# A linear attention and gated feed-forward kernel on one core: the diagonal term token-major from the seventh group on, a group's attention products in one visit of TensorE, two masked copies per group

## Chip, cores, metric

The kernel runs on one core of a Trainium2 chip. The metric is device time in microseconds (us) of one execution, lower is better. A core has TensorE (PE, matmuls; PEld is its weight load), VectorE (DVE), ScalarE (ACT), GpSimd (POOL) and SyncE (SP, which here issues every DMA).

## What is computed

Batch 4, 8 heads, 768 tokens, head width 48; r, k, v, w and u in float32, the feed-forward weights in float64. The reference, cut to what matters:

```python
for t in range(S):                                   # attention with a decaying state
    cur = einsum('bhd,bhe->bhde', u * k[t], v[t])    # the diagonal term: token t on itself
    y[t] = einsum('bhd,bhde->bhe', r[t], state + cur)
    state = w * state + einsum('bhd,bhe->bhde', k[t], v[t])
x = y laid out as (B, S, 384)
h = relu(x @ w_in)                                   # 384 -> 1024
gate = sigmoid(conv over 3 neighbouring tokens of h)
out = (h * gate) @ w_out                             # 1024 -> 384
```

## The kernel before, in words

**Attention.** Tokens go in chunks of C = 64 and groups of GT = 128 (two chunks); there are 6 groups per batch and NG = 24 in all, numbered g. The eight heads are four pairs (NP): one head of a pair lies on the upper partitions, the other on the lower ones, so most products come as two small matmuls side by side. Tiles with a number g % 3 hold three groups (NBUF).

For each group `prep` (L445) does this: it scales k and r in their channel-major form by powers of w (`KR`, on DVE); DMAs the scaled r into `RA` and `RB`, the moving operand of the output product; builds the diagonal term; and scales the token-major k, `KT`, into `KTA`/`KTB` (for g >= DK = 8 through an in-place product and two DMAs). The diagonal term of a token is the sum over the channels of r u k, one number for each token and head. Before, it comes in four steps: `KP` = k times r in channel-major form (512 columns, DVE or POOL); `qmm`, 32 matmuls of one column each that sum `KP` with the weights `uw` over the partitions into `psS` (L476 and L477); an ACT copy into `QQ`; and, for g >= DS = 2, a product of `QQ` with the identity `eye` that writes a diagonal matrix for all heads into `SC` (L298, class "dg").

`scores` (L504) makes the 64 x 64 products of k and r of a chunk in `psC` (32 matmuls, L513 and L514). For g >= DS one masked copy on DVE (COPY_PREDICATED, 128 partitions, L518) puts the part above the diagonal into `SC`, and two DMAs move `SC` into the two halves of `RA` and `RB`. For the first two groups POOL's affine_select (L498) writes the diagonal straight into `RA` and `RB`, and two masked copies of 64 partitions (L524) go there too.

`step(g, c)` (L529) is one chunk: `S`, the next state, 16 matmuls into `psS` (L536, L537), which two ACT copies take into `WW` (L543) where the next chunk's products read it; and `av`, the output of the chunk, 16 matmuls into `psY` (L550, L551). The last chunk of a batch has no `S`. `yout` copies `psY` out and lays it into `XT`, split into two float32r parts.

**Feed-forward.** 9 units of tokens (three of 254 to 258 in batch 0, then 384 each) times 8 blocks of 128 channels make 72 steps. `first` (L612, 9 matmuls into one of two `HP` banks) is followed by a chain that goes back and forth between ACT (ReLU L616, L617, sigmoid L623, rounding to `GH` L626) and DVE (two taps of the convolution L620, the gate L624), with the low part `GL` on DVE or POOL. `second` (L641, 9 matmuls into `PO`) comes three steps later. The weights arrive as float64 words and are turned into two float32r parts on ACT, DVE and POOL during the first third of the kernel.

**The order.** Every operation is entered in a `Plan` with an engine (or DVE and POOL to choose from, `tt("any", ...)`), an estimated duration and the tiles that it reads and writes. `late` gives each a due time, from the order of entry of PE's operations and a table of offsets OFF by class. `order` then schedules all of them on a model of the engines, earliest start first, most overdue first among those that are ready, and writes the instructions out in that order for each engine. For PE an operation of the kind in progress (feed-forward, or attention as a whole: ATT) gets a bonus of BON = 6 us, and leaving attention is charged SWITCH = 0.19 us. Groups are entered in `pieces`: at piece 3g `prep(g + 2)` and `scores(g + 1)`, then `step(g, 0)`, then `step(g, 1)`, `yout(g)` and `load(g + 3)`; so each third of a group is due at its own place between the feed-forward steps. In the steady part this gives visits of attention on PE such as q + av, S + sc and S + av, with feed-forward between them.

Of the kernel before, what the change touches and what calls it, by code (L numbers as in the profile page):

```python
# [5 lines left out]
F32 = mybir.dt.float32  # L6
# [4 lines left out]
ALU = mybir.AluOpType  # L11
# [2 lines left out]

DR = 2
DK = 8
DS = 2
LAG = 3
WPRE = 2
LEAD = 6  # L20
# [28 lines left out]
C = 64  # L49
# [13 lines left out]
class Plan:  # L63
# [6 lines left out]
    def __init__(self):  # L70
        self.ops = []
        self.last_w, self.last_r = {}, {}
        self.port = []

    def op(self, eng, dur, rd, wr, fn, cls="", x=0.0, port=False):
# [21 lines left out]
        self.port.append(port)  # L97
        return n

    def late(self):  # L100
        ops, n = self.ops, len(self.ops)
        late = [1e6] * n
        t = T0
        for i, (dur, x, pred, fn, cls) in enumerate(ops):
            if "pe" in dur and x:
                late[i] = t
                t += dur["pe"] * (1 + (SLOW if t < TS else 0.0))
        for i in reversed(range(n)):
            for j in ops[i][2]:
                d, x = ops[j][:2]  # L110
                m = min(d.values()) + LAT if "sp" not in d else d["sp"] + x + 1.5
                late[j] = min(late[j], late[i] - m)
        for i in range(n):
            late[i] -= OFF.get(ops[i][4], 0.0)
        return late

    def order(self):
# [17 lines left out]
        seq, where, when = [], [None] * n, [None] * n  # L135
        fill, hist = FILL, []
        lanes = [0.0] * 7
        att = False
        todo = n
        while todo:  # L140
            best = None
            for e in self.ENG:
                av = avail[e]
                if not av:
                    continue
                f = free[e]
# [12 lines left out]
                m = min(max(f, ready[i]) for i in av)
                lim = m + DELTA  # L160
                if e == "pe":
                    i = min((late[i] - (BON if (ops[i][4] in ATT) == att else 0.0), i) for i in av if ready[i] <= lim)[1]
# [8 lines left out]
            if e == "pe":  # L171
# [20 lines left out]
                if att and cls not in ATT:  # L192
                    free[e] += SWITCH
                att = cls in ATT
                s = max(s, free[e])
                k = int(s / self.TICK)
                if k > tick:
# [45 lines left out]


LAT, LPE = 0.18, 0.21
SLOWER, SHARED, SWITCH, XFER = 0.8, 1.25, 0.19, 1.45
ATT = ("th", "sc", "S", "av", "q")


def rwkv_ffn_kernel(tc, krd, krt, vt, wd, ut, w_in, conv_w, w_out, out):  # L250
# [4 lines left out]
    with ExitStack() as ctx:  # L255
# [11 lines left out]
        KTA, KTB = sb([112, NP, 2, D], F32, "KTA", NBUF), sb([128, NP, 2, D], F32, "KTB", NBUF)  # L267
        WW = sb([128, 2, NP, 2, D], F32, "WW", NBUF)
        WA, WB = [x[0:112, 0] for x in WW], [x[:, 1] for x in WW]
        KT = sb([128, NP, 2, D], F32, "KT", NBUF)  # L270
        KP = sb([112, NP, GT], F32, "KP", 2)
        QQ = sb([128, NP * 2], F32, "QQ", NBUF)
        YY = sb([128, NP, 2, GT], F32, "YY", 2)
# [19 lines left out]

        def tt(eng, n, rd, wr, cls="", **kw):
            d = {"dve": dve(n), "pool": pool(n)}
            if eng != "any":
                d = {eng: d[eng]}
            op(eng, d, rd, wr, lambda e: e.tensor_tensor(**kw), cls, port=True)  # L298
# [4 lines left out]

        wz = sb([128, 512], BF16, "wz")
        wc = sb([112, NP], F32, "wc")
        uc, uw = sb([112, NP], F32, "uc"), sb([112, NP], F32, "uw")
        mask = sb([128, C], I32, "mask")
        ident, eye = sb([112, D], F32, "ident"), sb([128, C], F32, "eye")
# [17 lines left out]
        if NW:  # L326
            op("pe", 0.2134 * NW, ["wz"], ["o2"], warm, "", 512 * NW)

        def load(g):
            i = g % NBUF  # L330
            dma([], [("KK", i), ("RR", i)], KR[i], krd[g], 0.45, 1.27, "ldK")
            dma([], [("KT", i)], KT[i], krt[g, :, 0], 0.45, 0.55, "ldT")
            dma([], [("Wv", i, "a")], WA[i][0:64], vt[g, 0:64, 0], 0.45, 0.27, "ldV")
            dma([], [("Wv", i, "b")], WB[i][64:128], vt[g, 64:128, 1], 0.45, 0.27, "ldV")

# [108 lines left out]

        def prep(g):  # L445
            i = g % NBUF
            k_t = KT[i]

            def c2(ap, n):
                return ap.unsqueeze(2).broadcast_to([n, NP, 2, C])  # L450
# [18 lines left out]
            kp = KP[g % 2]  # L469
            tt("any", 512, [("KK", i), ("RR", i)], [("KP", g % 2)], out=kp, in0=KK[i], in1=RR[i], op=ALU.mult)  # L470

            def qmm(e):
                for p in range(NP):
                    for c in range(2):
                        n, t = NP * D + 2 * p + c, slice(c * C, (c + 1) * C)
                        PE.matmul(psS[0:64, n:n + 1], kp[64:112, p, t], uw[64:112, p:p + 1], start=True, stop=True)  # L476
                        PE.matmul(psS[64:128, n:n + 1], kp[0:48, p, t], uw[0:48, p:p + 1], start=True, stop=True)  # L477
            op("pe", 0.4, [("KP", g % 2), ("uw", 0), ("uw", 64)], ["psAu", "psBu"], qmm, "q", 16)
            op("act", 0.2, ["psAu", "psBu"], [("QQ", i)], lambda e: A.copy(QQ[i], psS[:, NP * D:NP * D + 2 * NP]))
# [24 lines left out]
        def scores(g):  # L504
# [3 lines left out]
            def mm(e):  # L508
                for c in range(2):
                    for p in range(NP):  # L510
# [1 line left out]
                        n = (2 * p + c) * C  # L512
                        PE.matmul(psC[0:64, n:n + C], kk[64:112, p, t], rr[64:112, p, t], start=True, stop=True)  # L513
                        PE.matmul(psC[64:128, n:n + C], kk[0:48, p, t], rr[0:48, p, t], start=True, stop=True)  # L514
            op("pe", 0.5, [("KK", i), ("RR", i)], ["psAs", "psBs"], mm, "sc", 768)
            if g >= DS:
                sc = SC[g % 2].rearrange("q (a t) -> q a t", t=C)
                op("dve", 0.68, ["psAs", "psBs", "mask"], [("SC", g % 2)], lambda e: V.copy_predicated(  # L518
# [10 lines left out]
        def step(g, c):  # L529
            i = g % NBUF  # L530
            b, gi = divmod(g, GPB)
            if not (gi == GPB - 1 and c == 1):
                def smm(e):
                    for p in range(NP):
                        n = p * D
                        PE.matmul(psS[64:112, n:n + D], KTA[i][:, p, c, :], WA[i][:, p, c, :], start=True, stop=True)  # L536
                        PE.matmul(psS[0:48, n:n + D], KTB[i][:, p, c, :], WB[i][:, p, c, :], start=True, stop=True)  # L537
                j, cn = (i, 1) if c == 0 else ((i + 1) % NBUF, 0)
                op("pe", 0.2, [("KTk", i, "a"), ("KTk", i, "b"), ("KTd", i, "a", c), ("KTd", i, "b", c), ("KTd", i), ("Wv", i, "a"),
                              ("Wv", i, "b"), ("WS", i, c), ("Wz", i)], ["psAu", "psBu"], smm, "S", 720)  # L540
                for nm, T, ps, o in (("a", WA, psS, 64), ("b", WB, psS, 0)):
                    op("act", 0.21, ["psAu" if nm == "a" else "psBu"], [("WS", j, cn)] if nm == "a" else [("WS", j, cn)],
                       lambda e, T=T, ps=ps, o=o: A.copy(  # L543
                           T[j][o:o + 48, :, cn, :], ps[o:o + 48, 0:NP * D].rearrange("q (p d) -> q p d", p=NP)))
            t = slice(c * C, (c + 1) * C)

            def av(e):
                for p in range(NP):
                    n = p * GT + c * C
                    PE.matmul(psY[64:112, n:n + C], WA[i][:, p, c, :], RA[i][0:112, p, t], start=True, stop=True)  # L550
                    PE.matmul(psY[0:48, n:n + C], WB[i][:, p, c, :], RB[i][:, p, t], start=True, stop=True)  # L551
            op("pe", 0.25, [("Wv", i, "a"), ("Wv", i, "b"), ("WS", i, c), ("Wz", i), ("Rr", i, "a"), ("Rr", i, "b"), ("Rs", i, "a"), ("Rs", i, "b"), ("Rz", i)],
               ["psY"], av, "av", 960)

        def yout(g):
            b, gi = divmod(g, GPB)
# [203 lines left out]
```

## Time and profile before

| | |
|---|---|
| Runs of the kernel | 353.74, 355.93, 356.5 us; median 355.93 |
| The profiled execution | 356.31 us, its span on the core 354.6 us |
| Mean granted TensorE clock | 0.971 |
| Instructions | 10924 |
| DMA traffic | 46.62 MB in 28498 packets |

The profile is one execution taken by the hardware profiler. Times in it are us from the span's start, or ns where marked. A line of PE's timeline gives the start, the length, the line of the kernel, the operation and what it reads and writes; matmuls overlap, so the time that a series takes is read from start to start. A row of the groups gives line, engine, operation, shapes and count, then busy us and mean ns, then the engine's idle time ahead of them and what ended it. L298 is the helper `tt`, where nearly all elementwise products are issued, and L301 the helper for DMAs; there the tiles' names tell what it is.

### The profile page before, as it was taken

Reading aid. Unit: us, or ns where it says so; the run is one execution under the profiler, and the core shown is the slowest. Engines: PE = TensorE matmul, PEld = TensorE weight load, DVE = VectorE, ACT = ScalarE, POOL = GpSimd, SP = SyncE. Lnnn points to the kernel's source line nnn. Section 1 sums busy time; section 2 is a strip of 40 time slices with the busy share of each in tenths; the row PEclk is TensorE's granted clock in tenths of the full one; section 3 lists DMA queues with packets and bytes.
Section 4 is the critical chain, followed back from the end, with each engine's and each line's share of the span. In section 5 each row is a group of like instructions: output and inputs, shape, how many; then the busy total and the mean of one; then the engine's idle time right before and its main releaser. Section 6 shows DMA issues by size and latency. Waiting matters only on the chain.

```text
span 354.6 us, 10924 instructions
## 1 busy us (share of the span) xinstructions
PE 338.8 (96%) x4439; PEld 311.8 (88%) x4439; DVE 239.6 (68%) x387; ACT 215.4 (61%) x531; POOL 150.4 (42%) x159
## 2 busy tenths in 40 slices
PE   7899898859999999999999999999999999999996
PEld 3688787749999999999899999999989999999995
DVE  7969969898676777776765666566534665565560
ACT  5445685854575677465646674565555776676752
POOL 8878676397532224345326242424122031233330
PEclk9899989876999999999999999999999999999999
DMA  7947956776446436866655272457332300010101
GB/s 185 271 131 193 273 162 220 227 186 159 120 132 179 146 108 169 224 170 165 181 131 163 77 193 79 123 146 208 77 72 57 110 3 2 11 67 2 67 2 67
DMA packets 28498, 46.62 MB, mean 131 GB/s; under 512 B 5984, under 2 KB 18784, under 8 KB 28448
## 3 DMA queue, kind: packets, MB, share of 16 engines
q1 hardware_dynamic: 28448, 45.92, 47.3%
q8 instruction: 35, 0.57, 0.6%
q14 instruction: 15, 0.12, 0.1%
HBM read 26.77 MB, written 4.72 MB: 89 GB/s over the span
## 4 chain that ended last, share of the span: by engine, by line
PE 85%; DVE 8%; DMA 3%; issue 2%; ACT 2%; SPq 0%; DVEq 0%
PE PO L641 30%; PE HP L612 29%; PE psY L550 6%; PE psC L513 5%; PE psS L476 5%; PE psS L536 5%; PE PO L696 2%; DVE KR L298 2%; DMA KR<-in_krd_dram 2%; DVE TT L422 2%; DVE TT L424 1%; DMA RB<-SC 1%; PE psS L477 1%; PE psY L551 1%; PE psS L537 1%
## 5 line engine op out<-in xcount | busy, mean ns | idle before, releaser
L612 PE MATMUL HP<-XT,wi 128*128 128x386 f32 (+3 forms) x648 | 118.3, 328 | 4.2 <-DVE SG L624 3.6
L641 PE MATMUL PO<-GH,wo 128*128 128x384 f32 (+3 forms) x432 | 119.7, 333 | 0.6 <-ACT wo L430 0.5
L612 PEld LDWEIGHTS HP<-XT,wi 128*128 128x128 f32 x648 | 106.4, 194 | 6.2 <-DVE SG L624 4.5
L620 DVE SCALAR_TENSOR_TENSOR CV<-HP,cw,CV 128x384 f32<-128x384 f32 (+3 forms) x144 | 81.7, 569 | 31.5 <-ACT CV L617 29.8
L298 POOL TENSOR_TENSOR GL<-SG,GH 128x384 fp32r<-128x384 f32 (+3 forms) x46 | 49.2, 1069 | 116.4 <-ACT GH L626 95.0
L641 PEld LDWEIGHTS PO<-GH,wo 128*128 128x128 f32 x432 | 78.7, 192 | 3.8 <-ACT wo L430 0.7
L641 PE MATMUL PO<-GL,wo 128*128 128x384 f32 (+3 forms) x216 | 69.7, 322 | 0.0
L616 ACT ACTIVATE HP<-HP 128x386 f32<-128x386 f32 (+3 forms) x72 | 31.8, 441 | 38.4 <-PE HP L612 37.3
L624 DVE TENSOR_TENSOR SG<-HP,SG 128x384 f32<-128x384 f32 (+3 forms) x72 | 36.6, 509 | 26.9 <-ACT SG L623 26.2
L623 ACT ACTIVATE SG<-CV 128x384 f32<-128x384 f32 (+3 forms) x72 | 35.1, 488 | 29.2 <-DVE CV L620 28.9
L641 PEld LDWEIGHTS PO<-GL,wo 128*128 128x128 f32 x216 | 41.6, 193 | 0.0
L617 ACT ACTIVATE CV<-HP,cw 128x384 f32<-128x384 f32 (+3 forms) x72 | 39.3, 546 | 1.2
L298 DVE TENSOR_TENSOR KR<-KR,TKR 112x1024 f32<-112x1024 f32 (+1 forms) x26 | 34.7, 1340 | 6.7 <-DMA KR<-in_krd_dram 5.2
L626 ACT CAST GH<-SG 128x384 fp32r<-128x384 f32 (+3 forms) x72 | 34.1, 474 | 6.9 <-DVE SG L624 6.8
L543 ACT COPY WW<-psS 48x192 f32<-48x192 f32 x88 | 27.4, 311 | 17.5 <-PE psS L537 16.1
L476 PEld LDWEIGHTS psS<-uw,KP 48*64 48x64 f32 x384 | 24.1, 135 | 9.1 <-POOL KP L298 2.2
L550 PE MATMUL psY<-RA,WW 112*48 112x64 f32 x384 | 30.6, 224 | 0.0
L551 PE MATMUL psY<-RB,WW 128*48 128x64 f32 x384 | 30.6, 224 | 0.0
L476 PE MATMUL psS<-uw,KP 48*64 48x1 f32 x384 | 26.0, 194 | 4.2 <-DVE KP L298 1.7
L513 PE MATMUL psC<-KR 48*64 48x64 f32 x384 | 27.7, 223 | 0.7 <-DVE KR L298 0.7
L518 DVE COPY_PREDICATED SC<-mask,psC 128x512 f32<-128x512 int32 x22 | 16.3, 740 | 17.2 <-PE psC L514 13.8
L514 PE MATMUL psC<-KR 48*64 48x64 f32 x384 | 27.7, 223 | 0.0
(85 smaller groups left out, 528.1 us busy)
## 6 DMA issues: line engine op xcount, KB each, us to landing
KR<-in_krd_dram SPq DMA_DIRECT2D x24, 448.0 KB, 4.5
KT<-in_krt_dram SPq DMA_DIRECT2D x24, 192.0 KB, 4.0
WW<-in_vt_dram SPq DMA_DIRECT2D x48, 96.0 KB, 3.4
out_dram<-OS SPq DMA_DIRECT2D x18, 192.0 KB, 2.1
ST<-in_w_in_dram SPq DMA_DIRECT2D x8, 384.0 KB, 5.2
ST<-in_w_out_dram SPq DMA_DIRECT2D x8, 384.0 KB, 4.2
RA<-SC SPq DMA_DIRECT2D x22, 128.0 KB, 2.7
RB<-SC SPq DMA_DIRECT2D x22, 128.0 KB, 2.7
```

The lines of the kernel that those rows point to most:

```text
L298: op(eng, d, rd, wr, lambda e: e.tensor_tensor(**kw), cls, port=True)
L476: PE.matmul(psS[0:64, n:n + 1], kp[64:112, p, t], uw[64:112, p:p + 1], start=True, stop=True)
L513: PE.matmul(psC[0:64, n:n + C], kk[64:112, p, t], rr[64:112, p, t], start=True, stop=True)
L550: PE.matmul(psY[64:112, n:n + C], WA[i][:, p, c, :], RA[i][0:112, p, t], start=True, stop=True)
L551: PE.matmul(psY[0:48, n:n + C], WB[i][:, p, c, :], RB[i][:, p, t], start=True, stop=True)
L612: PE.matmul(hp, wi[a][:, j, fs], X[:, x, j, t], start=(j == 0 and k == 0), stop=(j == 2 and k == 2))
L617: op("act", act(n) + 0.05, [H_, "cw"], [("T", ti)], lambda e: A.activation(t1, hp[:, 1:n + 1], AF.Copy, scale=cw[:, 3 * f + 1:3 * f + 2]), ...
L620: op("dve", dve(n + 60), [H_, "cw"], [("T", ti)], lambda e, k=k: V.scalar_tensor_tensor(out=t1, in0=hp[:, k:n + k], scalar=cw[:, 3 * f + k ...
L623: op("act", act(n), [("T", ti)], [("SG", ti)], lambda e: A.activation(sg, t1, AF.Sigmoid))
L624: op("dve", dve(n), [H_], [("SG", ti)], lambda e: V.tensor_tensor(out=sg, in0=hp[:, 1:n + 1], in1=sg, op=ALU.mult), "GG")
L626: op("act", act(n), [("SG", ti)], [("GH", gi)], lambda e: A.copy(gh, sg))
L641: PE.matmul(PO[m][:, :n], wo[a][:, f, ms], g2[x], start=(f == 0 and k == 0), stop=(f == NF - 1 and k == 2))
```

## The change

- **Diagonal term.** For g >= DQ = 6 the load brings the token-major r beside k (`krt[g]` whole, `KT` has room for both), and `u`, repeated on all partitions, is loaded once with group 6 as `uu`. `KRT` multiplies r by k in place (384 columns), `KRU` by u (both on DVE or POOL), and a reduction on DVE over the 48 channels writes `QQ`. `KP`, the 32 one-column matmuls and ACT's copy remain for groups 0 to 5 alone.
- **Masked copies.** DS goes from 2 to 24, so the way of the first two groups (two affine_selects on POOL, two masked copies on DVE straight into `RA` and `RB`) serves all groups; the diagonal product into `SC` and the two DMAs from `SC` are gone.
- **Visits.** From group VIS = 2 on, `S` and `av` of both chunks of group g and `sc` of group g + 1 form a visit with one due time. Once PE has begun one it issues only its members until all are done. It begins when all that its members need from outside is done within VWAIT = 0.8 us, or when it is over 8 us overdue (SLACK).
- **The planner's numbers.** PE's durations for q, sc, S and av are 0.94, 0.94, 0.36 and 0.45 instead of 0.4, 0.5, 0.2 and 0.25; three kinds of PE work instead of two (MODE: feed-forward, q and sc, S and av), each change charged 0.095; DMA transfers are reckoned at 1.2 instead of 1.45 per unit. `ALONE` is empty, and so does nothing.

```diff
-DS = 2
+DS = 24
+DQ = 6
+VIS = 2
+SLACK = -8.0
+VWAIT = 0.8
...
+        for m in self.visits.values():
+            t = min(late[k] for k in m)
+            for k, i in enumerate(sorted(m, key=lambda i: VORD.index(ops[i][4]))):
+                late[i] = t + 1e-3 * k
...
+                if e == "pe":
+                    if cur is not None:
+                        av = [i for i in av if self.visit.get(i) == cur]
+                    else:
+                        c = []
+                        for i in av:
+                            v = self.visit.get(i)
+                            if v is not None and not (late[i] < SLACK + f or all(end_of[j] is not None and end_of[j] <= f + VWAIT for j in ext[v])):
+                                continue
+                            c.append(i)
+                        av = c
+                    if not av:
+                        continue
...
-                    i = min((late[i] - (BON if (ops[i][4] in ATT) == att else 0.0), i) for i in av if ready[i] <= lim)[1]
+                    i = min((late[i] - (BON if MODE.get(ops[i][4], 0) == mode else 0.0), i) for i in av if ready[i] <= lim)[1]
...
-SLOWER, SHARED, SWITCH, XFER = 0.8, 1.25, 0.19, 1.45
-ATT = ("th", "sc", "S", "av", "q")
+SLOWER, SHARED, SWITCH, XFER = 0.8, 1.25, 0.095, 1.2
+VORD = ("S", "sc", "av")
+MODE = {"th": 1, "sc": 1, "q": 1, "S": 2, "av": 2}
...
-        KT = sb([128, NP, 2, D], F32, "KT", NBUF)
+        KT = sb([128, 2, NP, 2, D], F32, "KT", NBUF)
...
+        uu = sb([128, NP, D], F32, "uu")
...
+            if g == DQ:
+                dma([], ["uu"], uu, ut, 0.45, 0.27, "ldU")
...
-            dma([], [("KT", i)], KT[i], krt[g, :, 0], 0.45, 0.55, "ldT")
+            if g < DQ:
+                dma([], [("KT", i)], KT[i][:, 0], krt[g, :, 0], 0.45, 0.55, "ldT")
+            else:
+                dma([], [("KT", i), ("RT", i)], KT[i], krt[g], 0.45, 1.1, "ldT")
...
-            k_t = KT[i]
+            k_t, r_t = KT[i][:, 0], KT[i][:, 1]
...
+            else:
+                tt("any", 384, [("KT", i)], [("RT", i)], "KRT", out=r_t, in0=r_t, in1=k_t, op=ALU.mult)
+                tt("any", 384, ["uu"], [("RT", i)], "KRU", out=r_t, in0=r_t, in1=uu.unsqueeze(2).broadcast_to([128, NP, 2, D]), op=ALU.mult)
+                op("dve", 0.46, [("RT", i)], [("QQ", i)], lambda e: V.tensor_reduce(
+                    out=QQ[i], in_=r_t.rearrange("q p c d -> q (p c) d"), axis=AX.X, op=ALU.add), "QQ", port=True)
...
-            op("pe", 0.5, [("KK", i), ("RR", i)], ["psAs", "psBs"], mm, "sc", 768)
+            op("pe", 0.94, [("KK", i), ("RR", i)], ["psAs", "psBs"], mm, "sc", 768, visit=vis(g - 1))
```

More of the change, by code (lines that the diff above doesn't have):

```diff
@@ L16 @@
 DK = 8
-DS = 2
+DS = 24
[3 more added lines that the diff above has]
+VWAIT = 0.8
+ALONE, AFTER = (), 0
 LAG = 3
@@ L73, in __init__, with op @@
         self.port = []
-    def op(self, eng, dur, rd, wr, fn, cls="", x=0.0, port=False):
+        self.visits, self.visit = {}, {}
+    def op(self, eng, dur, rd, wr, fn, cls="", x=0.0, port=False, visit=None):
         n = len(self.ops)
@@ L97, in op @@
         self.port.append(port)
+        if visit is not None:
+            self.visits.setdefault(visit, []).append(n)
+            self.visit[n] = visit
         return n
@@ L137, in order @@
         lanes = [0.0] * 7
-        att = False
+        mode, cur = 0, None
+        todo_v = {v: set(m) for v, m in self.visits.items()}
+        ext = {}
+        for v, m in self.visits.items():
+            inner = set(m)
+            for i in range(n):
+                if any(j in inner for j in ops[i][2]) and any(i in ops[k][2] for k in m):
+                    inner.add(i)
+            ext[v] = {j for k in m for j in ops[k][2]} - inner
+        end_of = [None] * n
         todo = n
@@ L191, in order @@
                 fill = fill and cls != "f2"
-                if att and cls not in ATT:
+                if MODE.get(cls, 0) != mode:
                     free[e] += SWITCH
-                att = cls in ATT
+                mode = MODE.get(cls, 0)
+                cur = self.visit.get(i)
+                if cur is not None:
+                    todo_v[cur].discard(i)
+                    if not todo_v[cur]:
+                        cur = None
                 s = max(s, free[e])
@@ L233, in order @@
             where[i], when[i] = e, (s, free[e])
+            end_of[i] = done
             for j in succ[i]:
@@ L295, in tt @@
             d = {"dve": dve(n), "pool": pool(n)}
+            if eng == "any" and (cls or (wr[0] if isinstance(wr[0], str) else wr[0][0])) in ALONE and len(plan.ops) > AFTER:
+                eng = "dve"
             if eng != "any":
@@ L327, in rwkv_ffn_kernel, with vis @@
             op("pe", 0.2134 * NW, ["wz"], ["o2"], warm, "", 512 * NW)
+        def vis(g):
+            return g if g >= VIS else None
         def load(g):
             i = g % NBUF
+            if g == DQ:
+                dma([], ["uu"], uu, ut, 0.45, 0.27, "ldU")
             dma([], [("KK", i), ("RR", i)], KR[i], krd[g], 0.45, 1.27, "ldK")
-            dma([], [("KT", i)], KT[i], krt[g, :, 0], 0.45, 0.55, "ldT")
+            if g < DQ:
+                dma([], [("KT", i)], KT[i][:, 0], krt[g, :, 0], 0.45, 0.55, "ldT")
+            else:
+                dma([], [("KT", i), ("RT", i)], KT[i], krt[g], 0.45, 1.1, "ldT")
             dma([], [("Wv", i, "a")], WA[i][0:64], vt[g, 0:64, 0], 0.45, 0.27, "ldV")
@@ L467, in prep, with qmm @@
                     dma([("RR", i)], wr, T[i][o:o + 48], RR[i][o:o + 48], 0.625, 0.27, "rmv")
[L469 to L479, printed above, removed]
+            if g < DQ:
+                kp = KP[g % 2]
+                tt("any", 512, [("KK", i), ("RR", i)], [("KP", g % 2)], out=kp, in0=KK[i], in1=RR[i], op=ALU.mult)
+                def qmm(e):
+                    for p in range(NP):
+                        for c in range(2):
+                            n, t = NP * D + 2 * p + c, slice(c * C, (c + 1) * C)
+                            PE.matmul(psS[0:64, n:n + 1], kp[64:112, p, t], uw[64:112, p:p + 1], start=True, stop=True)
+                            PE.matmul(psS[64:128, n:n + 1], kp[0:48, p, t], uw[0:48, p:p + 1], start=True, stop=True)
+                op("pe", 0.94, [("KP", g % 2), ("uw", 0), ("uw", 64)], ["psAu", "psBu"], qmm, "q", 16)
+                op("act", 0.2, ["psAu", "psBu"], [("QQ", i)], lambda e: A.copy(QQ[i], psS[:, NP * D:NP * D + 2 * NP]))
+            else:
[3 more added lines that the diff above has]
+                    out=QQ[i], in_=r_t.rearrange("q p c d -> q (p c) d"), axis=AX.X, op=ALU.add), "QQ", port=True)
             if g < DK:
@@ L538, in step @@
                 j, cn = (i, 1) if c == 0 else ((i + 1) % NBUF, 0)
-                op("pe", 0.2, [("KTk", i, "a"), ("KTk", i, "b"), ("KTd", i, "a", c), ("KTd", i, "b", c), ("KTd", i), ("Wv", i, "a"),
-                              ("Wv", i, "b"), ("WS", i, c), ("Wz", i)], ["psAu", "psBu"], smm, "S", 720)
+                op("pe", 0.36, [("KTk", i, "a"), ("KTk", i, "b"), ("KTd", i, "a", c), ("KTd", i, "b", c), ("KTd", i), ("Wv", i, "a"),
+                              ("Wv", i, "b"), ("WS", i, c), ("Wz", i)], ["psAu", "psBu"], smm, "S", 720, visit=vis(g))
                 for nm, T, ps, o in (("a", WA, psS, 64), ("b", WB, psS, 0)):
@@ L551, in av @@
                     PE.matmul(psY[0:48, n:n + C], WB[i][:, p, c, :], RB[i][:, p, t], start=True, stop=True)
-            op("pe", 0.25, [("Wv", i, "a"), ("Wv", i, "b"), ("WS", i, c), ("Wz", i), ("Rr", i, "a"), ("Rr", i, "b"), ("Rs", i, "a"), ("Rs", i, "b"), ("Rz", i)],
-               ["psY"], av, "av", 960)
+            op("pe", 0.45, [("Wv", i, "a"), ("Wv", i, "b"), ("WS", i, c), ("Wz", i), ("Rr", i, "a"), ("Rr", i, "b"), ("Rs", i, "a"), ("Rs", i, "b"), ("Rz", i)],
+               ["psY"], av, "av", 960, visit=vis(g))
         def yout(g):
```

## The prediction

> **What bounds the kernel now.** I read the page's busy times first, then the chain that ended last, then the busy times by stretch.
>
> ```profile
> PE 338.8 (96%) x4439; PEld 311.8 (88%) x4439; DVE 239.6 (68%) x387; ACT 215.4 (61%) x531; POOL 150.4 (42%) x159
> PE 85%; DVE 8%; DMA 3%; issue 2%; ACT 2%; SPq 0%; DVEq 0%
> ```
> ```profile
> 20.00:87.00 67.00, 58.49 (x948) 51.49 (x946) 59.25 (x90) 42.60 (x110) 46.88 (x47) 0.87 0.71 198
> 87.00:125.00 38.00, 38.00 (x651) 35.26 (x648) 26.20 (x46) 22.88 (x65) 13.51 (x14) 1.00 0.53 143
> 125.00:200.00 75.00, 75.00 (x1097) 69.86 (x1093) 51.52 (x85) 46.68 (x120) 31.20 (x29) 1.00 0.60 157
> 200.00:304.00 104.00, 104.00 (x1268) 97.32 (x1266) 60.67 (x100) 63.65 (x151) 28.56 (x25) 1.00 0.35 95
> 304.00:354.60 50.60, 47.26 (x281) 46.86 (x280) 24.86 (x42) 30.51 (x65) 13.30 (x13) 1.00 0.11 38
> ```
> The columns of the second view are the stretch, its length, busy time of PE, PEld, DVE, ACT and POOL, granted clock, DMA share and GB/s. Until 87 us DVE is the fullest engine (59.25 of 67 us, 88%) and PE has gaps. From 87 us on PE is busy for the whole of each stretch at full clock: a start-up on the vector engines, 217 us of PE with attention in it, and a tail of feed-forward alone. DVE there has 26.20 + 51.52 + 60.67 = 138.4 us of work in 217 (64%, at most 69% in one stretch). So whatever leaves PE after 87 us shortens the kernel one for one, as long as DVE keeps up.
>
> What attention costs PE is read from its timeline:
>
> ```profile
> 91.22 0.21 PE L476 MATMUL psS<-uw,KP 48*64 48x1 f32 x1
> ...
> 169.84 0.24 PE L536 MATMUL psS<-WW,KTA 112*48 112x48 f32 x1
> 170.33 0.27 PE L513 MATMUL psC<-KR 48*64 48x64 f32 x1
> 171.41 0.44 PE L641 MATMUL PO<-GH,wo 128*128 128x384 f32 x1
> ...
> 201.19 0.21 PE L476 MATMUL psS<-uw,KP 48*64 48x1 f32 x1
> 202.22 0.26 PE L550 MATMUL psY<-RA,WW 112*48 112x64 f32 x1
> ...
> 204.50 1.75 PE L612 MATMUL HP<-XT,wi 128*128 128x386 f32 x9
> 206.18 0.24 PE L536 MATMUL psS<-WW,KTA 112*48 112x48 f32 x1
> 206.68 0.44 PE L641 MATMUL PO<-GH,wo 128*128 128x384 f32 x1
> 206.96 0.34 PE L641 MATMUL PO<-GL,wo 128*128 128x384 f32 x1
> 210.05 0.24 PE L536 MATMUL psS<-WW,KTA 112*48 112x48 f32 x1
> 210.44 0.22 PE L550 MATMUL psY<-RA,WW 112*48 112x64 f32 x1
> 210.99 0.44 PE L641 MATMUL PO<-GH,wo 128*128 128x384 f32 x1
> ...
> 304.00 0.26 PE L550 MATMUL psY<-RA,WW 112*48 112x64 f32 x1
> ```
> Start to start: q takes 202.22 - 201.19 = 1.03 us though each of its matmuls has one column; S 0.39 (210.05 to 210.44). S alone takes 0.50 to the next feed-forward matmul, so 0.11 is spent leaving; S then av takes 0.94, so av is 0.44; sc takes 1.08 with leaving (170.33 to 171.41), 0.97 without. A feed-forward matmul takes (1.75 - 0.34)/8 = 0.176, so the nine from 204.50 end at 206.09: entering costs 0.09. The first one after a visit takes 0.28 (206.68 to 206.96) for 0.176: another 0.10. **Each visit of attention thus pays about 0.30 besides its work.** S to sc takes 0.49 for S to av's 0.39: a change between the two kinds inside a visit costs 0.10.
>
> **Part 1: q leaves PE from group 6 on.**
>
> ```profile
> 87.00:304.90 217.90, 17.42 (x256) 1.00 0.46 124
> ```
> This is line 476 alone: 256 matmuls on PE, 16 for each q, so 16 of the 24 groups' q stand behind 87 us. Groups 6 and 7 are among the 8 before, where PE isn't the bound, so I count nothing for them; 16 x 1.03 = **-16.5 us**. ACT's copy of q goes too, off the path.
>
> **Part 2: one visit for each group.** In PE's timeline behind 87 us, attention stands in 46 separate visits (from the q at 91.22 us to the av at 304.00, both quoted) for 18 groups' steps. They become 18: 28 x 0.30 = -8.4. Inside, I expect S, av, sc, S, av: the planner prefers the kind that it is in, and the second S needs the state of the first. That puts a change from sc back to S into 17 visits, +1.7. Together **-6.7 us**.
>
> The new wait is the second S on ACT's two copies of the state, with PE held until then. PE's whole queue stands behind it, and so ACT and DVE, who live on its feed-forward results. It has av and sc as cover: 0.39 + 0.44 + 0.97 and two changes of 0.10 make 2.0 us from the first S to the second.
>
> ```profile
> 206.79 0.31 ACT L543 COPY WW<-psS 48x192 f32<-48x192 f32 x1
> 207.13 0.58 ACT L617 ACTIVATE CV<-HP,cw 128x384 f32<-128x384 f32 x1
> 207.61 0.30 ACT L543 COPY WW<-psS 48x192 f32<-48x192 f32 x1
> ...
> 211.67 0.31 ACT L543 COPY WW<-psS 48x192 f32<-48x192 f32 x1
> ```
> For the S at 206.18 the second copy ended 1.73 us behind its start, with a feed-forward activation between the two; for the S at 210.05 it was 1.93. So the cover just holds: 0. Without it (sc put last) the second S could start after 0.8 us and would wait 0.9 to 1.1 in 18 visits, 18 us; that is a rival below. Nothing can be gained beyond hiding it.
>
> **Part 3: what the vector engines take on.**
>
> ```profile
> L298 POOL TENSOR_TENSOR KP<-KR 112x512 f32<-112x512 f32 x15 | 20.8, 1386 | 14.0 <-DVE KR L298 13.8
> L518 DVE COPY_PREDICATED SC<-mask,psC 128x512 f32<-128x512 int32 x22 | 16.3, 740 | 17.2 <-PE psC L514 13.8 <-POOL KP L298 3.4
> L298 POOL TENSOR_TENSOR SC<-eye,QQ 128x512 f32<-128x512 f32 x11 | 12.6, 1148 | 25.0 <-ACT QQ L479 25.0
> L298 POOL TENSOR_TENSOR KT<-KT,TH 128x384 f32<-128x384 f32 x9 | 10.3, 1147 | 9.3 <-DMA KT<-in_krt_dram 9.2
> L298 DVE TENSOR_TENSOR SC<-eye,QQ 128x512 f32<-128x512 f32 x11 | 8.8, 799 | 3.9 <-ACT QQ L479 3.9
> L298 DVE TENSOR_TENSOR KP<-KR 112x512 f32<-112x512 f32 x9 | 8.6, 957 | 0.0
> L298 DVE TENSOR_TENSOR KT<-KT,TH 128x384 f32<-128x384 f32 x7 | 4.5, 647 | 0.7 <-DMA KT<-in_krt_dram 0.7
> L498 POOL TENSOR_SCALAR_AFFINE_SELECT RA<-QQ 64x512 f32<-64x512 f32 x2 | 1.6, 812 | 0.1
> L524 DVE COPY_PREDICATED RB<-mask,psC 64x512 f32<-64x512 int32 x2 | 1.5, 733 | 0.1
> ```
> A masked copy of half the partitions takes as long as a whole one (733 against 740 ns), so two for one add 0.73 on DVE. For 16 groups in the PE-bound stretch: masked copies +11.7; the reduction, which the trace doesn't have, reads 384 columns: no more than KT's 0.65 with two inputs, and hardly under half of that (which would take 5 us from the total below); taken at 0.60: +9.6; the products with r and u are 32, and with half of them on DVE at 0.65 they add +10.4. Gone, in the shares that DVE had: the diagonal product 16/2 x 0.80 = -6.4 and KP 16 x 9/24 x 0.96 = -5.8. Net +19.5: **DVE has 158 us to do**. POOL gets two selects (32 x 0.8 = 26) and half of the products (16 x 1.15 = 18), and loses KP (10 x 1.39) and diagonals (8 x 1.15): +21 on 73.
>
> PE alone would now need 217 - 23.2 = 194 us, in which DVE would be 81% full. At 81% I don't expect a fixed order of instructions to run without waits. Bounds: nothing, if DVE can be as full as the 88% of 20 to 87 us; 158/0.69 - 194 = +35 if it can't be fuller than the 69% of the fullest stretch where PE set the pace. I take 79%, nearer to the first, since in those stretches DVE stood idle only because PE gave it no more: **+5 us**.
>
> **Part 4: start-up.** The second masked copies of groups 2 to 6 and the reductions and products of groups 6 to 8 fall before 87 us, where DVE is the bound: +3.6 (5 x 0.73) +1.8 +2.0, less diagonals and KP at the same shares as above (-2.0 -1.1), so about +4. Against it the hop of the scores by DMA is gone, two issues a group on SP's queue and a landing in 2.7 us, once on the chain:
>
> ```profile
> 33.64 3.82 DMA RB<-SC
> ...
> RA<-SC SPq DMA_DIRECT2D x22, 128.0 KB, 2.7
> ```
> I take **+3 us**, ends -1 and +8. The load of r beside k adds 192 KB for each of 18 groups (one DMA made longer), and u comes once, while 256 KB of moves go: nothing, with DMA at 60% or less behind 87 us. The planner's new durations for PE change its order everywhere; I count nothing for that, and the ends of this term cover it.
>
> **Sum**, against the profiled execution (span 354.6, own time 356.31, 0.4 above the median of 355.93): -16.5 - 6.7 + 5 + 3 = -15.2, a span of 339.4; from the median, **341 us**. No change, to a measurement here, is within 1%, 352.4 to 359.5.
>
> **A rule that speaks against it.**
>
> ```profile
> 57.31 1.21 DVE L298 TENSOR_TENSOR KR<-KR,TKR 112x1024 f32<-112x1024 f32 x1
> ...
> 69.28 2.06 DVE L298 TENSOR_TENSOR KR<-KR,TKR 112x1024 f32<-112x1024 f32 x1
> ...
> 70.20 1.98 POOL L298 TENSOR_TENSOR GL<-SG,GH 128x254 fp32r<-128x254 f32 x1
> ```
> The same product took 1.21 us and, with POOL at work beside it, 2.06. The Trainium skill (SBUF — State Buffer, section SBUF: two separate sides) says that DVE, when an operation has two SBUF inputs, and a GpSimd operation that reads SBUF hold one port pair by an exclusive lock, and the other blocks fully. The two KR rows agree with it in kind. My means are of rows that contain such blocking; by the rule the 21 us that POOL adds could block DVE for some of that time again, and by my estimate the +5 would be nearer +10.
>
> **Rivals.**
> - *Vector engines pace the rest (slower).* Place: 87 to 304 us, each step of the feed-forward waits in turn for ACT and DVE, and group work in DVE's queue delays it; products on POOL stretch DVE's by the KR rows' factor. It decides below 158/217 = 73% of DVE: at the 69% seen, 158/0.69 = 229, +12 on 217, with +3 at start-up 371. For it: 69% is never passed while PE is full. Against: 88% in start-up.
> - *The same, milder.* DVE at 76%: 208 us instead of 217, +3: 350.
> - *The visit waits inside* (sc not used as cover): -15.2 + 18 - 5 (DVE catches up meanwhile) = -2: 354, no change. Against it: the planner's order gives sc before the second S.
> - *Nothing is lost.* DVE at 81%, start-up unmoved: -23.2, 333.
>
> **How the numbers follow.** Forecast 0.62, nothing lost 0.13, mild 0.11, visit waits 0.07, slower 0.07. Faster is the sum of the first three, 0.86; same 0.07; slower 0.07. 331 to 352 holds the first three but for ends of the best case: 331 adds a start-up gained, 352 takes in the mild case with a longer start-up.
>
> **What would show it.** Line 476 with 96 matmuls (6 groups); some 18 visits behind the start-up, of about 3.1 us each with entering and leaving, with no gap before the second S; DVE at 75 to 83% between start-up and the last visit and PE still over 95% there; PE filling up at 88 to 92 us. Wrong if PE shows gaps of some us in all in the stretch with attention and they wait on DVE, or if visits are much longer than 3.1 us.

## The result, and the profile after

The changed kernel takes 341.46 us (median; 339.81 to 343.43) against 356.22 for the kernel before: a ratio of 0.9595, 95% interval 0.9521 to 0.9669. The forecast was 341. The total came out as told. The terms for the vector engines and the start-up did not, nor did the wait inside visits that was put at 0; their errors, of opposite sign, nearly cancelled, so that the total fits so well is luck.

The page of the changed kernel (span 339.6 us): busy times, PE's slices, the chain that ended last.

```profile
PE 313.7 (92%) x3824; PEld 293.4 (86%) x3824; DVE 258.5 (76%) x421; ACT 215.1 (63%) x513; POOL 181.0 (53%) x205
...
PE   8797888798999998799969999999999999999995
...
PE 55%; DMA 14%; DVE 13%; ACT 6%; SPq 5%; issue 4%; POOL 3%; DVEq 0%; POOLq 0%; ACTq 0%
```

PE lost 25 us of work, but its share fell from 96 to 92%, and it holds 55% of the chain instead of 85%: DMA, DVE, ACT and SP's queue came in. Of q's line 96 matmuls are left, those of 6 groups:

```profile
L531 PE MATMUL psS<-uw,KP 48*64 48x1 f32 x96 | 7.6, 205 | 5.8 <-ACT WW L603 4.0 <-DVE KP L343 1.3 <-DVE uw L439 0.5
```

Among the slices of 8.49 us from the sixteenth to the twenty-first (127 to 178 us) are now an 8, a 7 and a 6. The same by stretch (stretch, length, busy PE, PEld, DVE, ACT, POOL, granted clock, DMA share, GB/s):

```profile
87.00:125.00 38.00, 37.19 (x641) 34.80 (x641) 36.32 (x61) 25.99 (x69) 34.88 (x39) 1.00 0.66 184
125.00:200.00 75.00, 67.99 (x917) 64.45 (x916) 56.06 (x89) 44.42 (x106) 52.55 (x57) 0.93 0.64 179
200.00:290.00 90.00, 89.49 (x857) 86.66 (x856) 63.49 (x107) 60.41 (x132) 12.59 (x14) 1.00 0.15 43
290.00:339.60 49.60, 45.69 (x260) 45.36 (x259) 26.03 (x45) 28.95 (x63) 10.17 (x10) 1.00 0.10 37
```

From 125 to 200 us PE stands idle for 7 us and its clock is 0.93; before, it was full and at 1.00 there. The idle time isn't in the feed-forward: it is inside visits. All of PE's waits from 87 to 290 us (engine, tile and line, what it waited for, us in all, times, longest):

```profile
PE psS L596 <- ACT WW L603: 6.3, 4, 3.3
PE psY L611 <- DMA RB<-KR: 0.7, 1, 0.7
PE psY L610 <- DMA RA<-KR: 0.5, 1, 0.5
PE psY L611 <- ACT WW L603: 0.5, 1, 0.5
```

Here are an undisturbed visit and one that isn't, from PE's timeline (first matmul of each series; the one at 170.41 is the last of its `sc`):

```profile
88.22 0.24 PE L596 MATMUL psS<-WW,KTA 112*48 112x48 f32 x1
88.61 0.22 PE L610 MATMUL psY<-RA,WW 112*48 112x64 f32 x1
...
89.17 0.27 PE L573 MATMUL psC<-KR 48*64 48x64 f32 x1
...
90.24 0.24 PE L596 MATMUL psS<-WW,KTA 112*48 112x48 f32 x1
90.64 0.22 PE L610 MATMUL psY<-RA,WW 112*48 112x64 f32 x1
...
91.19 0.38 PE L701 MATMUL PO<-GH,wo 128*128 128x256 f32 x1
...
168.54 0.24 PE L596 MATMUL psS<-WW,KTA 112*48 112x48 f32 x1
...
170.41 0.22 PE L573 MATMUL psC<-KR 48*64 48x64 f32 x1
...
173.95 0.31 PE L596 MATMUL psS<-WW,KTA 112*48 112x48 f32 x1 [3.32 <-ACT WW L603]
...
175.62 4.73 PE L672 MATMUL HP<-XT,wi 128*128 128x386 f32 x14
```

The first is S, av, sc, S, av in 2.97 us from 88.22 to the feed-forward at 91.19, with the second S 2.02 after the first. The second has 7.08 us, 3.3 of them idle until ACT has copied the state. Behind 87 us there are 17 visits, from 88.22 to 280.84. Against the 2.96 us of an undisturbed one (2.61 at a batch's end, 1.38 for the last group), eight have no excess, nine have 0.19, 0.56, 0.19, 0.43, 1.72, 2.38, 4.12, 0.27 and 0.98 us: **10.8 us in all**, of which the waits above are 8.0. In the visit at 168.54, ACT did this:

```profile
171.22 0.52 ACT L683 ACTIVATE SG<-CV 128x384 f32<-128x384 f32 x1 [4.64 <-DVE CV L680]
172.20 0.51 ACT L631 CAST XT<-YY 128x384 fp32r<-128x384 f32 x1 [0.45 <-DMA YY<-YY]
172.74 0.31 ACT L603 COPY WW<-psS 48x192 f32<-48x192 f32 x1
173.06 0.52 ACT L631 CAST XT<-YY 128x384 fp32r<-128x384 f32 x1
173.59 0.31 ACT L603 COPY WW<-psS 48x192 f32<-48x192 f32 x1
```

and DVE this:

```profile
168.75 1.85 DVE L343 TENSOR_TENSOR KR<-KR,TKR 112x1024 f32<-112x1024 f32 x1 [1.87 <-DMA KR<-in_krd_dram]
170.52 1.13 DVE L680 SCALAR_TENSOR_TENSOR CV<-HP,cw,CV 128x384 f32<-128x384 f32 x2
```

Read backwards: the second state copy stands in ACT's queue behind a sigmoid that waits 4.64 us for the convolution on DVE. The convolution stands in DVE's queue behind the scaling of k and r of a later group, which waits 1.87 us for its load from HBM. The chain that ended last has that load:

```profile
161.30 7.43 DMA KR<-in_krd_dram
```

So a load that lands 7.4 us after its issue stops DVE, DVE stops ACT, and ACT stops PE, which by the rule of the visit may not do feed-forward in the meantime. The other long waits come by other ways. In the visit at 137.09 (2.30 us) ACT had stood still for a DMA that moves the finished output, so what ACT had in front of the state copies came late; in the visit at 127.88 PE itself waited for the two DMAs of the scaled r that the view of waits shows:

```profile
136.57 0.52 ACT L631 CAST XT<-YY 128x384 fp32r<-128x384 f32 x1 [2.36 <-DMA YY<-YY]
```

All three begin with a wait for a transfer. At the end of the idle stretch in the visit at 168.54 the clock drops:

```profile
171.00:174.00 3.00, 0.05 (x2) 0.05 (x3) 2.75 (x6) 2.28 (x6) 1.37 (x2) 0.87 0.40 100
174.00:177.00 3.00, 3.00 (x36) 2.86 (x37) 1.85 (x3) 2.24 (x6) 2.06 (x3) 0.50 0.92 267
177.00:180.00 3.00, 3.00 (x11) 3.00 (x11) 1.75 (x2) 1.07 (x3) 2.85 (x4) 0.50 0.90 211
```

After the idle stretch the granted clock is 0.50 for 6 us; the 18 feed-forward matmuls from 175.62 end at about 180.89, 5.27 us for 3.17. Behind the wait of 2.30 us in the visit at 137.09 the clock halves too, for 3.4 us, which costs about 1.7:

```profile
142.50:145.90 3.40, 3.40 (x11) 3.40 (x12) 2.78 (x4) 0.93 (x3) 2.16 (x3) 0.50 0.95 266
```

The start-up, in turn, became shorter. Here PE from 70 to 87 us in the kernel before and in the changed one:

```profile
70.00:80.00 10.00, 5.48 (x69) 4.67 (x67) 10.00 (x15) 5.93 (x17) 9.15 (x8) 0.78 0.73 196
80.00:87.00 7.00, 7.00 (x82) 6.57 (x82) 7.00 (x12) 3.02 (x8) 5.19 (x5) 0.58 0.65 173
```
```profile
70.00:80.00 10.00, 9.52 (x134) 8.86 (x132) 9.94 (x18) 6.97 (x19) 9.17 (x11) 1.00 0.46 135
80.00:87.00 7.00, 5.63 (x90) 5.01 (x86) 6.90 (x9) 4.76 (x15) 5.38 (x6) 1.00 0.49 154
```

DVE is full in both, but before, PE was busy for 5.48 of 10 us and then ran at 0.58 of the clock. Taking PE's instructions by line up to 87 us, the kernel before has 90 + 54 feed-forward matmuls behind it, the changed one 105 + 75:

```profile
0.00:87.00 87.00, 15.78 (x90) 0.88 0.73 202
0.00:87.00 87.00, 9.63 (x54) 0.88 0.73 202
```
```profile
0.00:87.00 87.00, 16.78 (x105) 0.90 0.74 210
0.00:87.00 87.00, 9.76 (x75) 0.90 0.74 210
```

36 matmuls of 254 to 258 columns (about 0.12 us each, 4.4 us) and group 6's visit less its scores (2.2): the start-up is ahead by about 6.6 us where I had forecast 3 behind.

**The balance behind 87 us.** PE's last matmul ended at 351.3 us before and at 335.7 after, 15.6 less. Forecast work saved -23.2 and work already done by 87 us -6.6 make -29.8, so 14.2 us were given back: 10.8 in visits, 2.1 and about 1.7 at half clock behind two of them, which is 0.4 more than there is to assign.

Some executions fall into a slower state of the chip: times below are medians of the fast ones, of which the changed kernel without visits has a single one, and the profiles of visits with transfers at 1.45 and of visits with all old numbers are of slow ones, so their stretches are not read.

### The profile page after: what moved, and what is told of

It reads as the page before. It is cut to its first block, busy times and chain, and to the rows that moved or that the text cites. A ratio compares the mean times of both kernels' runs of the same rounds, so it can differ in the third digit from the quotient of the medians.

```text
span 339.6 us, 9668 instructions
## 1 busy us (share of the span) xinstructions
PE 313.7 (92%) x3824; PEld 293.4 (86%) x3824; DVE 258.5 (76%) x421; ACT 215.1 (63%) x513; POOL 181.0 (53%) x205
## 4 chain that ended last, share of the span: by engine, by line
PE 55%; DMA 14%; DVE 13%; ACT 6%; SPq 5%; issue 4%; POOL 3%; DVEq 0%; POOLq 0%; ACTq 0%
PE HP L672 23%; PE PO L701 21%; SPq L346 5%; DMA ST<-in_w_in_dram 3%; PE psS L596 3%; DMA RB<-KR 3%; DVE CV L680 3%; DMA YY<-YY 3%; PE psC L573 2%; PE psY L610 2%; DMA KR<-in_krd_dram 2%; DVE TT L478 2%; DMA uc<-in_ut_dram 2%; DVE TT L476 2%; ACT WW L603 2%
## 5 line engine op out<-in xcount | busy, mean ns | idle before, releaser
L672 PE MATMUL HP<-XT,wi 128*128 128x386 f32 (+3 forms) x648 | 119.5, 335 | 4.4 <-DVE SG L684 4.2
L672 PEld LDWEIGHTS HP<-XT,wi 128*128 128x128 f32 x648 | 108.1, 198 | 7.7 <-DVE SG L684 6.4
L701 PE MATMUL PO<-GH,wo 128*128 128x384 f32 (+3 forms) x432 | 108.3, 319 | 0.7 <-ACT OS L708 0.7
L680 DVE SCALAR_TENSOR_TENSOR CV<-HP,cw,CV 128x384 f32<-128x384 f32 (+3 forms) x144 | 80.1, 568 | 19.7 <-ACT CV L677 18.3
L343 POOL TENSOR_TENSOR GL<-SG,GH 128x384 fp32r<-128x384 f32 (+3 forms) x36 | 35.8, 994 | 109.8 <-ACT GH L686 103.5
L701 PEld LDWEIGHTS PO<-GH,wo 128*128 128x128 f32 x432 | 75.9, 188 | 1.1 <-ACT OS L708 0.9
L684 DVE TENSOR_TENSOR SG<-HP,SG 128x384 f32<-128x384 f32 (+3 forms) x72 | 36.4, 508 | 17.4 <-ACT SG L683 16.9
L596 PE MATMUL psS<-WW,KTA 112*48 112x48 f32 x352 | 25.5, 217 | 8.1 <-ACT WW L603 7.9
L343 DVE TENSOR_TENSOR GL<-SG,GH 128x384 fp32r<-128x384 f32 (+3 forms) x36 | 23.1, 641 | 12.5 <-ACT GH L686 11.7
L596 PEld LDWEIGHTS psS<-WW,KTA 112*48 112x48 f32 x352 | 20.0, 129 | 14.5 <-ACT WW L603 9.6
L610 PE MATMUL psY<-RA,WW 112*48 112x64 f32 x384 | 31.7, 226 | 0.5 <-DMA RA<-KR 0.5
```

The costliest lines, as they stand in the source:

```text
L672: PE.matmul(hp, wi[a][:, j, fs], X[:, x, j, t], start=(j == 0 and k == 0), stop=(j == 2 and k == 2))
L680: op("dve", dve(n + 60), [H_, "cw"], [("T", ti)], lambda e, k=k: V.scalar_tensor_tensor(out=t1, in0=hp[:, k:n + k], scalar=cw[:, 3 * f + k ...
L684: op("dve", dve(n), [H_], [("SG", ti)], lambda e: V.tensor_tensor(out=sg, in0=hp[:, 1:n + 1], in1=sg, op=ALU.mult), "GG")
L701: PE.matmul(PO[m][:, :n], wo[a][:, f, ms], g2[x], start=(f == 0 and k == 0), stop=(f == NF - 1 and k == 2))
```

## The experiments

The theory after the traces: (1) taking q off PE pays more than its PE time, since it also frees the start-up; (2) fullness of DVE cost nothing; (3) visits cost what they save, because they hold PE while loads are late. Rivals stand in the expectations. Each run was timed against the kernel before in three rounds; before was 356.79, 356.13 and 357.75 us in the three sets, so between runs of different sets the ratios are compared too. Each edit makes the planner order everything anew, so a difference of a few us between two versions also holds what that order brings.

The expectations speak of the start of the twelfth feed-forward step on PE and put it at 95 us before and 86 after. These are two different steps: 95.41 is where the thirteenth series on `HP` starts in the kernel before, 86.22 where the twelfth starts in the changed one. Like with like the changed kernel is 3.8 us ahead by this mark, not 9 (twelfth 90.04 and 86.22, thirteenth 95.41 and 91.65). The table has the twelfth series, and the feed-forward matmuls that PE had behind it by 87 us, each from one profiled execution:

| Kernel | Matmuls by 87 us | Twelfth series starts |
|---|---|---|
| Before | 144 | 90.04 |
| Changed | 180 | 86.22 |
| Changed, q on PE | 156 | 90.82 |
| Changed, one copy | 185 | 85.28 |
| Before, new numbers alone | 153 | 88.57 |
| Before, diagonal term alone | 189 | 85.80 |
| Before, copies alone | 146 | 93.74 |
| Before, diagonal term and copies | 189 | 85.53 |
| The same from group 8 on | 143 | 94.16 |
| The same from group 4 on | 184 | 85.35 |

### Undoing one part of the changed kernel

```diff
-VIS = 2
+VIS = 99
```

> The changed kernel without visits: q off PE, two masked copies and the planner's numbers stay. Theory (being held inside a visit costs 10.8 us of waits, more than the 6.7 us that fewer visits save): 341.5 + 6.7 - 10.8 = 337, and anything up to 341 fits. Rival (what the second S waits for is late for everybody, and would stop PE at another place): 341.5 + 6.7 = 348 with PE gaps as long as before. 344.5 lies between the two.

333.61 us; three more runs, at a mean granted clock of 0.962 to 0.969 where this one had 0.985, took 339.11 to 340.31. All are on the theory's side of 344.5, and 1 to 8 us under the changed kernel's median; what the visits cost is not settled closer than that. In the run of 333.61 us PE's waits behind 87 us are these:

```profile
PE HP L672 <- DVE SG L684: 3.4, 6, 1.2
PE PO L701 <- POOL GL L343: 1.9, 1, 1.9
PE psS L596 <- ACT WW L603: 1.1, 1, 1.1
```

The wait for the state shrank from 6.3 to 1.1 us, and some 5 us of waits moved to the feed-forward, 6.4 in all for 8.0: a part of the lateness meets PE wherever it stands, as the rival said. There are 26 separate visits without any rule that makes them, not 46.

```diff
-DQ = 6
+DQ = 24
```

> The changed kernel with q on PE for all 24 groups (KP, 32 one-column matmuls, ACT's copy), visits and two masked copies stay. Theory (q costs PE 1.03 us a group one for one): 16 x 1.03 = 16.5 more, and up to 4.8 for q standing outside the visits, less up to 5 for the relief of DVE and POOL: 353 to 362. Rival (the products and the reduction on DVE and POOL cost nearly what PE saves): under 348.

370.39 us, ratio 1.0433 (1.0342 to 1.0525): slower than the kernel before, and 8 us beyond the theory's range. The rival is out. The forecast 16.5 can't be all that q costs. Here 15 q stand behind 87 us (15.5 us); 24 fewer feed-forward matmuls are done by then (2.9); and PE's waits behind 87 us are 18.5 us in place of 8.0. That comes to about the 28.9 us between the two kernels. A part of the waits stands in visits in which q, sc, S, av, S, av follow each other and take 4.8 us from 241 us on, where their work is under 4:

```profile
PE psS L596 <- ACT WW L603: 8.3, 9, 1.4
PE HP L672 <- DVE SG L684: 6.8, 3, 3.7
```

```diff
-DS = 24
+DS = 2
```

> The changed kernel with one masked copy into SC and two DMAs a group, and the diagonal product. Theory (the start-up was 7 us shorter because the hop by DMA and its issues are gone): the twelfth step of the feed-forward on PE starts some 5 to 8 us later than at 86 us, and the time is 345 to 350. Rival (the start-up gained by the planner's new numbers): the twelfth step within 2 us of 86, time 339 to 343, with DVE some 12 us less busy.

347.37 us, ratio 0.9728 (0.9623 to 0.9832). The time is the theory's, but its reason is wrong: the twelfth step begins at 85.28 us, no later than the 86.22 of the changed kernel, so the start-up did not come from the copies. What one copy costs comes later.

```diff
-DS = 24
-DQ = 6
-VIS = 2
+DS = 2
+DQ = 24
+VIS = 99
```

> The kernel before with the planner's new durations of PE, three kinds of PE work and the DMA transfer number alone; the work is that of before. Theory (the masked copies shortened the start-up): 354 to 358, start-up as before. Rival (the numbers did it): 347 to 351, the twelfth feed-forward step at 86 to 89 us instead of 95.

360.94 us, ratio 1.0156 (1.0070 to 1.0242): some 4 us slower, less than 2%, and outside both ranges. The twelfth step at 88.57 us is 1.5 earlier than before, with 9 more matmuls done by 87 us: little of the 36 that the changed kernel gained. That left the diagonal term.

### Adding parts to the kernel before

Here the diagonal term's lines of the change (`DQ`, `uu`, the longer load, `KRT`, `KRU`, the reduction) and, or, `DS` were put into the kernel before, with nothing else of the change.

```diff
+DQ = 6
...
-            kp = KP[g % 2]
...
+            if g < DQ:
...
+            else:
+                tt("any", 384, [("KT", i)], [("RT", i)], "KRT", out=r_t, in0=r_t, in1=k_t, op=ALU.mult)
```

> The kernel before with only the token-major diagonal term from group 6 on; one masked copy and two DMAs a group, no visits, the old numbers of the planner. Theory now (q costs PE 16.5 us behind 87 us, and q, KP and their chain cost the start-up 7 to 9 us besides, as the run with q on PE showed): 330 to 338, twelfth feed-forward step at about 87 us. Rival (the start-up was shortened by the copies and the numbers together, and q alone gives no more than its 16.5): 339 to 343, twelfth step at 94 to 96 us.

335.25 us, ratio 0.9386 (0.9314 to 0.9459), in the theory's range; twelfth step at 85.80 us, 4.2 earlier than before, and 45 more matmuls by 87 us. The diagonal term alone gives 20.9 us, more than the whole change.

```diff
-DS = 2
+DS = 24
```

> The kernel before with only two masked copies and two selects a group in place of the diagonal product, one copy and two DMAs; q stays on PE everywhere. Theory (the copies by themselves load DVE in the start-up by 0.73 us a group and give little back): 356 to 362. Rival (the hop by DMA was a cost of its own, worth the 6 us that the changed kernel lost with one copy): 349 to 353.

355.85 us, ratio 0.9996 (0.9955 to 1.0037): no change, just under the theory's 356 and well off the rival's range.

> The kernel before with the diagonal term and the two masked copies, without visits and with the old numbers of the planner. Theory (visits and new numbers add nothing to the other two parts): 336 to 342, as the changed kernel without visits (339.3). Rival (the new numbers help once q is gone, since they keep PE's attention together): 345 or more.

**330.51 us, ratio 0.9273 (0.9200 to 0.9345)**, 5.5 us under the theory's range and far from the rival's: this version, half of the change, beats both kernels. The copies that gave nothing alone give 4.7 us once q is gone. Its stretch from 125 to 200 us, where the changed kernel lost 7 us, and all that PE waited for behind 87 us:

```profile
125.00:200.00 75.00, 75.00 (x921) 70.64 (x920) 63.26 (x100) 48.38 (x114) 59.80 (x62) 1.00 0.64 182
```
```profile
PE psC L526 <- DVE RB L537: 0.4, 1, 0.4
```

PE is busy for 75.00 of 75 us while DVE is at 63.26, 84%. So DVE at 84% did not make PE wait here. PE's attention stands in 34 visits here, of 2.02 (S, av, sc) and 0.94 us (S, av) for the most part, none with a wait inside worth naming.

### The planner's numbers

```diff
-VIS = 2
+VIS = 99
...
-SLOWER, SHARED, SWITCH, XFER = 0.8, 1.25, 0.095, 1.2
+SLOWER, SHARED, SWITCH, XFER = 0.8, 1.25, 0.095, 1.45
```

> The changed kernel without visits and with DMA transfers reckoned at 1.45 per unit again. Theory (the new number lets loads be planned too close, so that late k and r stop DVE and through it PE): 2 to 5 us under the run without visits, 334 to 337. Rival (lateness of loads matters only inside a visit that holds PE): 338 to 341.

334.12 us, ratio 0.9355 (0.9292 to 0.9418; runs from 332.25 to 334.62). It lies in the theory's range, but that range was drawn from 339; against the 333.61 us of the same kernel with transfers reckoned at 1.2 nothing is gained. So a price of the transfer number without visits is not shown. From 330.51 to 334.12 it is PE's durations, its kinds and the charge for a change that differ.

```diff
-SLOWER, SHARED, SWITCH, XFER = 0.8, 1.25, 0.095, 1.2
+SLOWER, SHARED, SWITCH, XFER = 0.8, 1.25, 0.095, 1.45
```

> The changed kernel, visits and all, with DMA transfers reckoned at 1.45 per unit again. Theory (the waits inside visits come from k that lands later than planned: DVE stops for it, ACT behind DVE, and the state copy behind ACT's next feed-forward operation): the waits in the visits fall from 10.8 us to under 5, time 333 to 338. Rival (being held in a visit costs by itself, whenever the loads come): waits of 9 us or more, 340 to 343.

336.42 us, ratio 0.9388 (0.9337 to 0.9439): in the theory's range by time, 5.0 us under the changed kernel, and the two intervals don't meet. With visits, then, the transfer number matters. How much waiting stayed in the visits is open, as its profile isn't read.

The visits on top of the version of 330.51 us, all numbers as before:

```diff
+VIS = 2
```

> The kernel before with the diagonal term, the two masked copies and the visits, all numbers of the planner as before: the visits alone, against 330.5 us without them. Theory (with loads in time, visits save their 0.30 us each but leave the planner less to choose, so little is left): 328 to 333. Rival (a visit holds PE idle whatever the numbers): 335 or more.

348.46 us, ratio 0.9747 (0.9699 to 0.9795): the rival, by far. Visits alone cost 18.0 us there (16.9 by the ratios). With PE's new durations no cost is clear (336.42 against 334.12, with intervals that overlap), and with all new numbers it is the 1 to 8 us of above. In no setting did they pay. Other values of VWAIT and SLACK were not tried. That this is PE being held idle, as in the visit at 168.54, is shown for the changed kernel and argued for this one.

### The start-up

From the version of 330.51 us:

```diff
-DQ = 6
+DQ = 8
```

> The kernel with diagonal term and copies alone (330.5 us) with the token-major diagonal only from group 8 on, so that the q of groups 6 and 7 is on PE again, in the start-up. The prediction counted these two at nothing: 330 to 332 by that. Theory now (the start-up's 9 us came from taking q and its chain out of it): 335 to 340, with the twelfth feed-forward step at 90 to 95 us instead of 85.5.

339.74 us, ratio 0.9482 (0.9420 to 0.9545), in the theory's range: 9.2 us for the q of groups 6 and 7 (7.4 by the ratios of the two sets), which the prediction priced at nothing and which take 2.1 us of PE. The start of the twelfth step in the version of 330.51 us, then in this one:

```profile
85.53 1.24 PE L625 MATMUL HP<-XT,wi 128*128 128x258 f32 x9
```
```profile
94.16 1.35 PE L625 MATMUL HP<-XT,wi 128*128 128x258 f32 x9
```

and the stretch from 40 to 87 us in the same order:

```profile
40.00:87.00 47.00, 42.87 (x564) 38.73 (x560) 44.16 (x77) 36.05 (x94) 39.10 (x42) 0.89 0.71 206
```
```profile
40.00:87.00 47.00, 40.66 (x489) 36.80 (x485) 37.08 (x65) 29.67 (x77) 33.29 (x38) 0.78 0.69 195
```

With the two q's PE is idle for 2.2 us more, and a mean clock of 0.78 in place of 0.89 is some 5 us more lost at half clock. With the 2.1 us of the q's that is 9.3 us; the two profiled executions are 8.5 apart, and 46 feed-forward matmuls fewer are done by 87 us. So the loss is idle time and half clock in the start-up, well beyond q's own time. One piece of the idle time is a wait that the other lacks:

```profile
PE psS L484 <- DVE KP L299: 1.3, 1, 1.3
```

The rest, which the planner's other order brings, is not pinned to an operation. DVE isn't what fills up: it is busy for less of the stretch here, 37.08 us for 44.16.

```diff
-DQ = 6
+DQ = 4
```

> The same with the token-major diagonal from group 4 on. Theory (each q in the start-up costs some 3 us there): 325 to 329. Rival (the start-up is then bound by DVE and the loads, which get more to do): 330 or more.

334.37 us, ratio 0.9337 (0.9299 to 0.9375): in the rival's range. Two groups earlier gives no further gain; whether it costs anything isn't clear (3.9 us by the medians, 2.3 by the ratios, whose intervals overlap). What stops the gain was not tried.

## Why the prediction was right, step by step

- **What bounds it: right.** PE set the time behind 87 us; what left PE there came off the end, and in the version of 330.51 us it did so almost one for one.
- **q off PE, -16.5: right in kind, too small.** Line 531 has 96 matmuls, so the 16 q behind 87 us are gone. The step that failed is "where PE isn't the bound, so I count nothing for them": the q of groups 6 and 7 are worth 7 to 9 us, as the run from group 8 on showed. DVE was nearly full there, and I took that to mean that PE's waits cost nothing; but PE's idle time was followed by stretches at half clock, and q, which waits for KP (1.4 us once in the kernel before), added to it.
- **One visit a group, -6.7: work right, wait wrong.** 17 visits stand behind 87 us, 14 of them in the order S, av, sc, S, av, and an undisturbed one takes 2.96 us to the next feed-forward matmul, 3.15 with entering and the slow first one after it, as worked out (3.1). The step that failed is "So the cover just holds: 0". It was 10.8 us, and 3.8 more at half clock behind two of the visits. I had read the cover from two visits in which ACT's queue moved. The state copy waits not for the two copies' own time but for whatever ACT has in front of it, and under a rule that holds PE, a late transfer reaches PE through that queue: a load through DVE's and ACT's in the longest wait, a move of output through ACT's in the next. I had named the queue behind PE, but not the one in front of the copy on ACT. And the saving was smaller than 28 visits: without q, and with no rule, 34 (the version of 330.51 us) or 26 visits (the changed kernel without the rule) remain of 46.
- **DVE at 79%, +5: the wrong place.** DVE had 92.4 us to do from 87 to 200 us (36.32 + 56.06 of 113, 82%), near the 81% feared, yet the version of 330.51 us ran PE full with DVE at 84%. So the term should have been about 0. The choice was also not worked out exactly: 79% gives 158/0.79 - 194 = +6, not +5. The rival in which the vector engines pace the rest falls with it, at 84% against its limit of 73.
- **The rule on the shared port.** By the Trainium skill (SBUF — State Buffer, section SBUF: two separate sides) POOL's added reads should have blocked DVE's two-input products further. In the changed kernel DVE's products of 128 x 384 with u or k took 544 and 558 ns where POOL was at rest and 551 to 1073 ns in the five cases beside POOL at work, so blocking is there in kind. In the version of 330.51 us PE was full beside DVE at 84% and POOL at 59.80 of 75 us, so there it did not reach the time. In the changed kernel the KR product that holds up the visit at 168.54 took 1.85 us beside POOL, and 1.22 at 126.5 us without, so up to 0.6 us of that wait can be its doing.
- **Start-up, +3: wrong sign.** It was about -6.6, and that comes from the diagonal term: with it alone 189 matmuls are done by 87 us for 144 before, with the copies alone 146, with the new numbers alone 153, and with q back on PE 156 for the changed kernel's 180.
- **Sum.** -16.5 - 6.7 held; 0 and +3 should have been about +14 (visits that took longer and the clock behind two of them) and -6.6, and +5 about 0. The forecast of 8 given back met 7.6 (14.2 - 6.6). It was right by that balance, which is luck, and not by its parts.
- **The new numbers of the planner, counted at nothing:** PE's durations, kinds and the charge cost 3.6 us without visits (330.51 to 334.12), the shorter DMA transfers about 5 with visits (336.42 to 341.46) and nothing that shows without. That they put loads too late fits the transfers seen ahead of the waits; it isn't shown that these waits shrink with the longer ones.

## What to carry to other kernels

Taking small matmuls off a full PE paid more than their PE time, because in the start-up waits on their chain and stretches at half clock went with them. Before pricing a wait at nothing because its cover is long enough, look at what stands in front of the releasing operation on its engine, and follow that one's wait too. A rule that forbids an engine to do other work can turn a late transfer into that engine's idle time; try each part of a combined change alone, since here half of it (0.927) beat the whole (0.960).

## What the runs showed of the hardware

An idle stretch of 3.3 us on PE was followed by 6 us at a granted clock of 0.50, which cost another 2.1 us; one of 2.3 us was followed by 3.4 us at 0.50, about 1.7 us. The reduction of 384 columns to 8 took 544 ns, below the 600 assumed. The two products of the same shape have means of few cases:

```profile
L538 DVE TENSOR_REDUCE QQ<-KT 128x8 f32<-128x384 f32 x18 | 9.8, 544 | 3.1 <-POOL KT L343 3.1
...
L343 DVE TENSOR_TENSOR KT<-KT,uu 128x384 f32<-128x384 f32 x4 | 3.6, 893 | 0.0
L343 DVE TENSOR_TENSOR KT<-KT 128x384 f32<-128x384 f32 x3 | 1.7, 571 | 0.8 <-DMA KT<-in_krt_dram 0.8
```
